# Pooled attention then top-1 experts: other SBUF places for V and scores, Q ahead of K at the start, w2 split after the tokens

## The chip, the cores and the metric

The program runs on one core of a Trainium2 chip. The metric is the device time of one execution in microseconds. Before the change it is 1212.16 us, the median of three runs (1210.98 to 1213.45).

## What is computed

Attention over 8 batches x 8 heads x 1152 tokens x 64, with queries pooled in pairs, then a top-1 mixture of 8 experts over the 4608 pooled tokens. All arrays are float32.

```python
q_pool = q.reshape(B, H, S // 2, 2, D).mean(axis=3)
scores = scale * np.matmul(q_pool, k.transpose(0, 1, 3, 2))
attn = softmax(scores)                     # over the 1152 keys
x = (attn @ v) -> (4608, 512)
e = argmax(x @ w_gate)                     # one expert for a token
out = gate * (np.maximum(x @ w1[e], 0) @ w2[e])
```

## The kernel before, in words

**Attention.** The work goes by pairs of heads: 8 batches x 4 pairs. For a pair, `load_pair` loads K (`kn`), Q (`qn`) and V (`vn`) by SP's queue. Neighbouring queries are added into `qp` (line 491; by POOL, for the first pair by DVE), ACT lays K beside itself as `kp` (line 495), TensorE turns both (lines 512 and 518) into PSUM tiles `st`, and ACT copies these to `kT` and `qT` (lines 524 and 529). The 576 pooled queries are handled in two halves of 288. For each half, `scores` makes 9 chunks of 128 keys: a product into `st` (line 556) and an eviction by DVE to the score tile `s` with the running extreme (line 561). There are two `st` tiles, four `s` tiles and three `vn` tiles. When the 9 chunks are done, DVE and TensorE make one bias of them (lines 582, 579, 585), ACT takes the exponential in three parts (line 589), POOL folds the sums (line 635), and `values` multiplies with V (line 660), after which ACT and DVE put the result in `xT` (lines 665 and 666).

**Routing.** After each batch, `row_sums` and `routing` make the logits from `xT` and the router's weights `wg` (line 735), rank the tokens and write the tokens and lists to DRAM.

**Experts.** The tokens are worked in slots of up to 384: two early slots that are known after the last batch but one, then the 8 experts by rank. For a slot, POOL gathers token rows (line 940), `turn_tokens` weighs them (lines 1100, 1101), transposes them on DVE (`xt`, line 1104) and splits them into a high and a low part (`xh` on ACT, line 1108; `xl` on DVE, line 1063). `split_weights` does the same with w1 and w2, four pieces each (`w1h`, `w2h` on ACT, line 1125; `w1l`, `w2l` on DVE, line 1063). `first_products` (line 1157) and `second_products` (lines 1188, 1218) each do three products for one, and `hh` and `hl` (lines 1164, 1166) are the layer between.

**What sets the order.** The `Flow` class plans all this: each step has an engine, a guessed duration, a key and predecessors; `emit` runs a small event simulation with these guesses and issues the steps in the order that comes out. The engines execute that order strictly, each its own; a step's key only shifts it in the plan.

**Memory.** Attention's `kT`, `qT`, `vn` and `fold` are in the pool `rt`, the score tiles in `sp`; both lie on the right side of SBUF. When the last attention step has been issued, `swap_units` closes these pools and opens those of the experts over the same bytes. A new tile then waits for the last readers of the old tiles that lay there.

**The opening.** SP issues K of the first pair, then Q in two transfers; `WARM` products of ones (line 1261) run on TensorE; ACT's queue issues four small loads of `wg`. The lines on which the order there rests are

```python
k0 = f.carry("SP", 480, lambda: load(kn.t, kb), key + K_LOAD, (), [kn], 2600)
q0 = f.carry("SP", 960, load_q, key + K_LOAD, (), [qn], 2600)
piece(key, [8], [0, 1, 2, 3, 4, 5], done(k1, q1))
piece(key + 4, [0, 1, 2, 3, 4, 5, 6, 7], [], done(k1))
```

Of the kernel before, what the change touches and what calls it, by code (L numbers as in the profile page):

```python
# [9 lines left out]
F32 = mybir.dt.float32  # L10
# [54 lines left out]
FILL = 3  # L65
WARM = 2
SWITCH = 110
CALM, CALM_X = 700, 500
# [198 lines left out]
def kernel(  # L267
# [76 lines left out]
    wg_src = w_gate.rearrange("(a s d) e -> s d a e", s=2, d=D)  # L344
    for s in range(2):
        for half in range(2):
            nc.scalar.dma_start(out=wg[s * D:(s + 1) * D, :, half, (2 * half + s) * NE:(2 * half + s + 1) * NE], in_=wg_src[s])
    rev = const.tile([QP, NE], F32, name="rev")
# [67 lines left out]
    def open_attention(exact, base, pairs, units):  # L416

        o = Pools()
        o.wk = base.enter_context(tc.tile_pool(name="wk", bufs=1 if exact else 2))
        o.ps_m = base.enter_context(tc.tile_pool(name="ps_m", bufs=5 if exact else BANKS, space=PSUM))  # L420
        o.ld = pairs.enter_context(tc.tile_pool(name="ld", bufs=1))
        right = {} if exact else dict(side="right")
        o.rt = units.enter_context(tc.tile_pool(name="rt", bufs=1 if exact else 2, **right))
        o.sp = units.enter_context(tc.tile_pool(name="sp", bufs=2 if exact else UNITS, **right))
        o.ps_s = units.enter_context(tc.tile_pool(name="ps_s", bufs=1 if exact else S_BUFS, space=PSUM))
        o.exact = exact
        o.turned, o.before = [], None
        return o
# [30 lines left out]
    def load_pair(o, f, key, b, hp):  # L459
# [13 lines left out]
        load = lambda out, src: nc.sync.dma_start(out=out, in_=src)  # L473
        k0 = f.carry("SP", 480, lambda: load(kn.t, kb), key + K_LOAD, (), [kn], 2600)
        first = not o.exact and b == 0

        def load_q():
            x.q_loads = [load(qn.t[i * D:(i + 1) * D], qb[i * BL:i * BL + D]) for i in range(2)]

        def load_v():  # L480
            ins = load(vn.t, heads(v, b, hp).rearrange("h (p c) d -> p h c d", p=P))
            if first:
                for other in x.q_loads:
# [3 lines left out]
        q0 = f.carry("SP", 960, load_q, key + K_LOAD, (), [qn], 2600)  # L487
        x.v = f.carry("SP", 480, load_v, key + (-30 if opening else K_V), done(q0) if first else done(o.before), [vn], 2600)
        o.before = x.v
        e, eng, ns = ("DVE", nc.vector, dve) if opening else ("POOL", nc.gpsimd, pool)  # L490
        q1 = f.add(e, ns(2 * NJ * D), lambda: eng.tensor_tensor(  # L491
            qp.t.rearrange("p j h d -> p h j d"), qn.t[:, :, :, 0, :], qn.t[:, :, :, 1, :], ALU.add), key + K_POOL,
            done(q0), [qn, qp])

        k1 = f.add("ACT", act(2 * NC * D), lambda: nc.scalar.copy(kp.t.rearrange("p c h d -> p h c d"), kn.t), key + K_POOL,
                   done(k0), [kn, kp])
        key += K_PIECE
        x.k, x.q = {}, {}

        QH = QP // 2  # L500
        assert QP - D == BL and QH + (D - QH) == D and (1 + NJ) * D <= 512

        def piece(key, ks, qs, after):

            pt = hold_of("st", lambda h: o.ps_s.tile([P, 2, 512], F32, **h.own("st")))
            nk = len(ks)

# [12 lines left out]

            s = f.add("PE", 31 * 2 * (nk + len(qs)), turn, key, after, [pt, *([kT, kp] if ks else []), *([qT, qp] if qs else [])], ROWS)
            o.turned.append(s)
            if ks:
                e = f.add("ACT", act(nk * P) - 44, lambda: nc.scalar.copy(
                    kT.t[:, ks[0] * P:(ks[0] + nk) * P].rearrange("p (c r i) -> p r c i", r=2, i=D),
                    pt.t[:, :, :nk * D].rearrange("p r (c i) -> p r c i", i=D)), key, done(s), [pt, kT])
                x.k.update((c, done(e)) for c in ks)
            if qs:
                e = f.add("ACT", act(NQ) - 44, lambda: nc.scalar.copy(
                    qT.t.rearrange("p (j r i) -> p r j i", r=2, i=QH),  # L530
                    pt.t[:, :, nk * D:(nk + NJ) * D].rearrange("p r (j i) -> p r j i", i=D)[:, :, :, D - QH:]),
                    key, done(s), [pt, qT])
                x.q.update((half, done(e)) for half in range(2))

        piece(key, [8], [0, 1, 2, 3, 4, 5], done(k1, q1))
        piece(key + 4, [0, 1, 2, 3, 4, 5, 6, 7], [], done(k1))
        return x

# [574 lines left out]

    def split_weights(m, f, x, kind, key, step, pool_bits):

# [125 lines left out]
    with ExitStack() as cm, ExitStack() as units, ExitStack() as pairs:  # L1241
# [14 lines left out]
        hold = []  # L1256
        pw = bank(o)

        def warm_up():
            for i in range(WARM):  # L1260
                nc.tensor.matmul(pw.t, ones, ones.unsqueeze(1).broadcast_to([P, 4, P]), start=True, stop=True)

        if WARM:
            f.add("PE", 2900 * WARM, warm_up, -1000, holds=[pw])
        for b in range(B):
# [11 lines left out]
            outs = routing(o, f, key, b, xT, rec, sums, outs, hold)  # L1277
            if b == B - 2:
# [11 lines left out]
        for i, ns in enumerate(((EARLY_N,),) * EARLY + RANKS):  # L1290
# [3 lines left out]
            for j, n in enumerate(ns):  # L1294
# [82 lines left out]
```

## Time and profile before

| what | value |
|---|---|
| median of three runs | 1212.16 us (1210.98 to 1213.45) |
| profiled execution, own time | 1203.37 us |
| its span | 1201.8 us |
| TensorE busy | 1159.8 us, 97% of the span |
| VectorE / ScalarE / GpSimd busy | 783.2 / 636.6 / 848.7 us |
| granted TensorE clock, mean | 0.993 |

Times in rows are microseconds from the span's start. "PE" is TensorE's products, "PEld" its weight loads, "DVE" VectorE, "ACT" ScalarE, "POOL" GpSimd, "SPq" the queue that issues transfers. A bracket at a row's end gives the idle time of that engine before it and what ended it. TensorE's products are pipelined, so the durations of neighbours overlap.

### The profile page before, as it was taken

How to read it: one execution, taken by the hardware profiler on the slowest of the kernel's cores; microseconds unless marked ns; L12 is line 12 of the kernel's file. 1: busy time of each engine (PE TensorE's matmuls, PEld its weight loads, DVE VectorE, ACT ScalarE, POOL GpSimd, SP SyncE). 2: the span in 40 equal slices, each digit the busy share in tenths (PEclk: the TensorE clock that was granted, in tenths of full speed). 3: DMA queues.
4: the chain of work that ended last, by engine and by line, in shares of the span. 5: the costliest groups of instructions: out<-in, count | busy, mean ns of one | idle time of the engine just before them, and what ended most of it. 6: DMA issues, size and time to landing. Idle time of an engine off the chain costs nothing.

```text
span 1201.8 us, 33990 instructions
## 1 busy us (share of the span) xinstructions
PE 1159.8 (97%) x14185; PEld 818.4 (68%) x14185; DVE 783.2 (65%) x2147; ACT 636.6 (53%) x784; POOL 848.7 (71%) x468
## 2 busy tenths in 40 slices
PE   7999999999999999999999998998999999999996
PEld 3555565555565555565555554997898989999985
DVE  5767867867867767877867965984454644536440
ACT  3666666666666567566657555443342433525440
POOL 1989899899899999899999525365666665641010
PEclk9999999999999999999999998999999999999998
DMA  7554525424524433534435333673353434525320
GB/s 195 118 139 112 109 56 144 109 60 115 135 64 122 98 88 102 119 87 124 99 90 125 81 120 96 148 237 113 97 160 90 153 116 129 153 85 185 112 91 20
DMA packets 77491, 138.12 MB, mean 115 GB/s; under 512 B 11274, under 2 KB 34706, under 8 KB 77329
## 3 DMA queue, kind: packets, MB, share of 16 engines
q1 hardware_dynamic: 66528, 116.19, 36.4%
q0 software_dynamic: 9712, 19.64, 5.7%
q8 instruction: 113, 1.85, 0.7%
q14 instruction: 50, 0.40, 0.1%
q10 hardware_dynamic: 1088, 0.03, 0.1%
HBM read 115.04 MB, written 21.02 MB: 113 GB/s over the span
## 4 chain that ended last, share of the span: by engine, by line
PE 46%; POOL 4%; issue 4%; DVE 3%; DMA 2%; ACT 1%; SPq 0%; POOLq 0%; DVEq 0%; ACTq 0%
PE ph L1157 17%; PE py L1218 12%; PE m L660 5%; PE py L1188 5%; PE st L556 5%; POOL fold L635 3%; PE sums L630 1%; DMA qn<-in_q_dram 1%; DVE s L561 1%; POOL qp L491 1%; PE sums L644 1%; DMA xr<-x_runs,ix 0%; PE m L1207 0%; ACT s L589 0%; PE st L512 0%
## 5 line engine op out<-in xcount | busy, mean ns | idle before, releaser
L561 DVE TENSOR_SCALAR_CACHE_REDUCE s<-st 128x576 f32<-128x576 f32 x576 | 419.7, 753 | 156.8 <-PE st L556 152.7
L589 ACT ACTIVATE s<-s,bias 128x1728 f32<-128x1728 f32 x192 | 320.6, 1729 | 167.9 <-DVE bias L585 160.7
L556 PE MATMUL st<-qT,kT 64*64 64x288 f32 x4608 | 364.9, 412 | 8.5 <-DVE s L561 6.9
L660 PE MATMUL m<-s,vn 64*64 64x288 f32 x4608 | 355.8, 405 | 0.0
L556 PEld LDWEIGHTS st<-qT,kT 64*64 64x64 f32 x4608 | 162.2, 133 | 146.5 <-DVE s L561 60.5
L660 PEld LDWEIGHTS m<-s,vn 64*64 64x64 f32 x4608 | 174.3, 133 | 86.5 <-issue 2.6
L635 POOL TENSOR_TENSOR fold<-s 128x1728 f32<-128x1728 f32 x58 | 224.4, 3869 | 7.0 <-ACT s L589 6.8
L635 POOL TENSOR_TENSOR fold<-fold,s 128x1728 f32<-128x1728 f32 x58 | 224.7, 3875 | 1.3
L940 POOL DMA_INDIRECT xr<-x_runs,ix x99 | 109.9, 1110 | 89.5 <-PE st L556 24.9
L1157 PE MATMUL ph<-xh,w1h 128*128 128x384 f32 (+6 forms) x480 | 151.5, 316 | 6.4 <-ACT xh L1108 6.0
L1157 PE MATMUL ph<-xl,w1h 128*128 128x384 f32 (+6 forms) x480 | 150.0, 313 | 1.1 <-DVE xl L1063 1.1
L1157 PE MATMUL ph<-xh,w1l 128*128 128x384 f32 (+6 forms) x480 | 149.5, 311 | 0.0
L1226 POOL DMA_INDIRECT out_dram<-y,rec x41 | 45.6, 1113 | 142.1 <-ACT hh L1164 46.7
L1166 DVE SCALAR_TENSOR_TENSOR hl<-ph,hh 128x384 fp32r<-128x384 f32 (+5 forms) x100 | 54.9, 549 | 107.8 <-ACT hh L1164 107.5
L1164 ACT ACTIVATE hh<-ph 128x384 fp32r<-128x384 f32 (+5 forms) x100 | 48.7, 487 | 133.4 <-PE ph L1157 133.3
L1157 PEld LDWEIGHTS ph<-xh,w1h 128*128 128x128 f32 x480 | 91.4, 190 | 9.3 <-ACT xh L1108 6.5
L1157 PEld LDWEIGHTS ph<-xl,w1h 128*128 128x128 f32 x480 | 91.4, 190 | 2.5 <-DVE xl L1063 1.8
L1157 PEld LDWEIGHTS ph<-xh,w1l 128*128 128x128 f32 x480 | 91.1, 190 | 0.0
L1218 PE MATMUL py<-w2h,hh 128*128 128x512 f32 x224 | 88.6, 395 | 0.0
L1218 PE MATMUL py<-w2h,hl 128*128 128x512 f32 x224 | 88.3, 394 | 0.0
L1218 PE MATMUL py<-w2l,hh 128*128 128x512 f32 x224 | 88.0, 393 | 0.0
L839 POOL DMA_INDIRECT lists<-re,di x48 | 46.2, 962 | 53.0 <-PE m L660 18.5
(186 smaller groups left out, 1464.7 us busy)
## 6 DMA issues: line engine op xcount, KB each, us to landing
raw<-in_moe_w_dram SPq DMA_DIRECT2D x80, 512.0 KB, 4.3
qn<-in_q_dram SPq DMA_DIRECT2D x64, 384.0 KB, 5.7
kn<-in_k_dram SPq DMA_DIRECT2D x32, 576.0 KB, 4.9
vn<-in_v_dram SPq DMA_DIRECT2D x32, 576.0 KB, 4.5
x_runs<-row SPq DMA_DIRECT2D x96, 99.0 KB, 2.1
xr<-x_runs,ix POOLq DMA_INDIRECT x99, 3.2
x_runs<-empty SPq DMA_DIRECT2D x4, 297.0 KB, 10.2
xq<-x_runs,ix POOLq DMA_INDIRECT x49, 2.7
```

The lines of the kernel that those rows point to most:

```text
L556: made = nc.tensor.matmul(pt.t[to, h, :HQ], x.kT.t[up, c * P + i * D:c * P + (i + 1) * D], x.qT.t[up, cols], start=True, stop=True, tile_p ...
L561: nc.vector.tensor_scalar(s.t[:, c], pt.t[:, :, :HQ], -SCALE, None, op0=ALU.mult, op1=ALU.min, accum_out=mx.t[:, c:c + 1],)
L589: nc.scalar.activation(s.t[:, c0:c0 + n], s.t[:, c0:c0 + n], AF.Exp, bias=bias.t, scale=-1.0)
L635: add = lambda to, a, b: nc.gpsimd.tensor_tensor(to, a, b, ALU.add)
L660: made = nc.tensor.matmul(pa[i].t[cs, :HQ], x.vn.t[up, h, c, :], s.t[up, c, h], start=c == 0, stop=c == NC - 1, tile_position=(up.start, c ...
L839: ins = nc.gpsimd.indirect_dma_start(out=lists, out_offset=bass.IndirectOffsetOnAxis(ap=di.t[:, j:j + 1], axis=0), in_=re.t[:, j, :], in_o ...
L940: return nc.gpsimd.indirect_dma_start(out=x.xr[i // NQD].t[:, i % NQD, :], out_offset=None, in_=xg, in_offset=bass.IndirectOffsetOnAxis(ap ...
L1157: made = nc.tensor.matmul(view()[:, i, :], a[:, c, fp], b[:, c, :n], start=c == 0 and k == 0, stop=c == NDC - 1 and k == 2)
L1164: a = f.add("ACT", act(nb * n) - 44, lambda fs=fs, view=view: nc.scalar.activation(hidden(m)[0][:, fs, :n], view(), AF.Relu), at - 20, don ...
L1166: d = f.add("DVE", dve(nb * n), lambda fs=fs, view=view: nc.vector.scalar_tensor_tensor(hidden(m)[1][:, fs, :n], view(), 0.0, hidden(m)[0] ...
L1188: made = nc.tensor.matmul(py.t[:, :n], a[:, c % 2, ds], b[:, c, :n], start=c == 0 and k == 0, stop=c == NFC - 1 and k == 2)
L1218: made = nc.tensor.matmul(py.t[:n], a[:, c, hs], b[:, c % 2, :], start=c == 0 and k == 0, stop=c == NFC - 1 and k == 2)
```

## The change

Five things are changed. (1) The router's weights are loaded by SP after the first pair, not by ACT's queue at the start. (2) The V tiles get a pool of their own, `vp`, opened after the score tiles, and the four score tiles are laid down at once in the order 3, 2, 1, 0. (3) In the first pair, the first half of Q is loaded first, then K in two parts (chunks 0 to 3 and 4 to 8), then Q's second half. The additions of Q, the copies of K, the turns and the copies after them go by the same parts, on DVE, POOL and ACT. (4) Small products of ones fill TensorE's time between these parts. (5) An expert's w2 is split only after its first tokens have been turned.

```diff
+FILL_W, FILL_Q, FILL_K = 2, 3, 2
...
+    def load_router():
...
-            nc.scalar.dma_start(out=wg[...], in_=wg_src[s])
+                nc.sync.dma_start(out=wg[...], in_=wg_src[s])
...
+        o.vp = o.rt if exact else units.enter_context(tc.tile_pool(name="vp", bufs=1, **right))
+        if not exact:
+            for i in reversed(range(UNITS)):
+                o.sp.tile([P, NC, 2, HQ], F32, name=f"s_{i}", bufs=1)
...
-        x.vn = vn = tile_of(o, "vn", [P, 2, NC, D], bufs=3, pool=o.rt)
+        x.vn = vn = tile_of(o, "vn", [P, 2, NC, D], bufs=3, pool=o.vp)
...
+        if opening:
+            parts = slice(0, 4), slice(4, NC)
+            q_in = [f.carry("SP", 1200, lambda: load_q(half_j[0]), key + K_LOAD, (), [qn], 1700)]
+            k_in = [f.carry("SP", 480, lambda cs=cs: load(kn.t[:, :, cs], kb[:, :, cs]), key + K_LOAD + 1 + cs.start, (), [kn], 1300)
+                    for cs in parts]
+            q_in.append(f.carry("SP", 1200, lambda: load_q(half_j[1]), key + K_LOAD + 10, (), [qn], 1700))
+            q1 = [pooled(e, js, done(p)) for e, js, p in zip(("DVE", "POOL"), half_j, q_in)]
+            k1 = [beside("ACT", slice(0, 2), done(k_in[0])), beside("DVE", slice(2, 4), done(k_in[0])), beside("ACT", parts[1], done(k_in[1]))]
+            q0 = q_in[1]
...
+            if fill:
+                f.add("PE", 230 * fill, lambda: o.warm(fill, 1), key, [s] if s else (), [o.pw])
...
+        if opening:
+            piece(key, [], [0, 1, 2], done(q1[0]), FILL_Q)
+            piece(key + 1, [0, 1, 2, 3], [], done(*k1[:2]), FILL_K, True)
+            piece(key + 2, [4, 5, 6, 7, 8], [], done(k1[2]))
+            piece(key + 22, [], [3, 4, 5], done(q1[1]))
...
-                      key + step * j, done(got[j]), [raw[j], w[j]])
+                      key + step * j, [*done(got[j]), *after], [raw[j], w[j]])
...
+        f.add("PE", 3300, lambda: (warm(WARM, 4), warm(FILL_W, 1)), -1000, holds=[o.pw])
...
+                    router = f.carry("SP", 2600, load_router, 1, outs, [], 1500)
...
-                    w.w2, w.w2_ready = split_weights(m, f, w, "w2", at, 10, 0)
+                    w.w2, w.w2_ready = split_weights(m, f, w, "w2", at, 10, 0, x.turned)
```

Line numbers of the changed file are some 30 to 36 higher. Three places where the order of instructions shows it follow.

TensorE at the very start, before (`m` is the bank of the products of ones, `st` a PSUM tile, `kp` and `qp` K and Q ready to be turned):

```order
L1261 MATMUL m_222<-ones 128x512 x2
L512 MATMUL st_232<-ident,kp_230 128x64 x16
L512 MATMUL st_257<-ident,kp_230 128x64 x2
L518 MATMUL st_257<-ident,qp_253 128x48
L518 MATMUL st_257<-ident,qp_253 128x64
...
L556 MATMUL st_278<-qT_276,kT_251 64x288 x4
L556 MATMUL st_283<-qT_276,kT_251 64x288 x4
```

and now (`kp_333` is K of the second pair):

```order
L1297 MATMUL m_225<-ones 128x512 x2
L1297 MATMUL m_225<-ones 128x128 x2
L543 MATMUL st_240<-ident,qp_238 128x48
...
L1297 MATMUL m_225<-ones 128x128 x3
L537 MATMUL st_255<-ident,kp_252 128x64 x8
L1297 MATMUL m_225<-ones 128x128 x2
L592 MATMUL st_270<-qT_250,kT_266 64x288 x4
L592 MATMUL st_275<-qT_250,kT_266 64x288 x4
L537 MATMUL st_286<-ident,kp_252 128x64 x10
...
L592 MATMUL st_335<-qT_250,kT_266 64x288 x4
L543 MATMUL st_344<-ident,qp_238 128x48
...
L537 MATMUL st_352<-ident,kp_333 128x64 x16
L592 MATMUL st_369<-qT_250,kT_266 64x288 x4
```

The first score product now follows half of Q and four chunks of K; the rest of K comes after two products, Q's second half and K of the second pair after eight.

DVE where attention ends and the first slot's tokens are turned, with what each row waits for (`xt` is the transposed token tile, `m_2` the result of the last half but one), before:

```order
L666 TENSOR_TENSOR xT_1_9171<-xT_1_9171,m_2_10080 128x288 [waits PE_49,Activation_49]
L1104 STREAM_TRANSPOSE xt_0_10259<-xr_0_9768 128x4x4x32 [waits DMAHW5_49,PE_49]
L1104 STREAM_TRANSPOSE xt_1_10264<-xr_1_9877 128x4x4x32
L1063 TENSOR_TENSOR w1l0_10262<-raw_0_9713,w1h0_10261 128x1024 [waits DMAHW0_49,Activation_49]
L1063 TENSOR_TENSOR xl_10267<-xt_0_10259,xh_10266 128x4x128 [waits Activation_49]
```

and now:

```order
L702 TENSOR_TENSOR xT_1_9195<-xT_1_9195,m_2_10104 128x288 [waits PE_49,Activation_49]
L1140 STREAM_TRANSPOSE xt_0_10284<-xr_0_9792 128x4x4x32
L1140 STREAM_TRANSPOSE xt_1_10289<-xr_1_9901 128x4x4x32
L1099 TENSOR_TENSOR w1l0_10287<-raw_0_9737,w1h0_10286 128x1024 [waits DMAHW3_49,Activation_49]
L1099 TENSOR_TENSOR xl_10292<-xt_0_10284,xh_10291 128x4x128 [waits Activation_49]
```

The order is the same; the transpose no longer waits for TensorE and a transfer. On ACT the second piece of w1 (`w1h1`) loses its wait for TensorE in the same way.

ACT where the third slot begins (`y` is a result of the slot before, `xh` the high part of the new tokens), before:

```order
L1236 COPY y_11076<-py_11028 128x512
L1125 CAST w2h_11089<-raw_10768 128x1024
L1125 CAST w2h_11102<-raw_10787 128x1024
L1125 CAST w2h_11117<-raw_10859 128x1024
L1236 COPY y_11123<-py_11069 128x512
L1125 CAST w2h_11128<-raw_10921 128x1024
L1108 CAST xh<-xt_11141 128x4x128
```

and now:

```order
L1272 COPY y_11101<-py_11053 128x512
L1272 COPY y_11134<-py_11094 128x512
L1144 CAST xh<-xt_11139 128x4x128
L1161 CAST w2h_11159<-raw_10793 128x1024
L1161 CAST w2h_11162<-raw_10812 128x1024
L1161 CAST w2h_11175<-raw_10884 128x1024
L1200 ACTIVATE hh<-ph_11152 128x384
```

The slot's last token tile is now cast ahead of all four pieces of w2; on DVE its weighing, transpose and low part stand ahead of them likewise.

## Rows read from the trace of the kernel before

**Rows 1.** Stretches: length, busy PE PEld DVE ACT POOL, clock, DMA, GB/s.

```profile
0.00:50.00 50.00, 41.23 (x538) 19.72 (x542) 30.20 (x150) 24.61 (x24) 25.43 (x21) 1.00 0.57 148
...
150.00:200.00 50.00, 49.49 (x842) 29.48 (x842) 33.60 (x98) 31.64 (x30) 49.06 (x19) 1.00 0.36 85
...
700.00:750.00 50.00, 44.76 (x651) 25.18 (x646) 32.01 (x84) 26.59 (x32) 24.72 (x24) 0.95 0.35 105
...
800.00:850.00 50.00, 45.52 (x218) 40.33 (x217) 26.06 (x50) 16.15 (x26) 29.33 (x28) 0.97 0.38 114
```

**Rows 2.** Order of time in the opening: start, duration, engine, line.

```profile
0.97 0.44 SPq L473 DMA_DIRECT2D kn<-in_k_dram  x1
...
1.28 3.78 PE L1261 MATMUL m<-ones 128*128 128x512 f32 x4 [1.28 <-DVE ones L322]
...
5.41 1.15 ACT L495 COPY kp<-kn 128x1152 f32<-128x1152 f32 x1 [2.94 <-DMA kn<-in_k_dram]
...
7.86 1.01 ACT L524 COPY kT<-st 128x1024 f32<-128x1024 f32 x1 [1.30 <-PE st L512]
...
9.84 0.96 DVE L491 TENSOR_TENSOR qp<-qn 128x768 f32<-128x768 f32 x1 [5.48 <-DMA qn<-in_q_dram]
...
10.86 0.91 PE L518 MATMUL st<-ident,qp 48*128 48x48 f32 x12 [2.93 <-DVE qp L491]
...
12.66 5.93 PE L556 MATMUL st<-qT,kT 64*64 64x288 f32 x48 [0.90 <-ACT qT L529]
...
24.18 0.29 DVE L585 TENSOR_REDUCE bias<-st 128x1 f32<-128x128 f32 x1
```

**Rows 3.** Score products on TensorE, 12.6 to 18.7 us: busy, mean ns.

```profile
L556 PE MATMUL st<-qT,kT 64*64 64x288 f32 x48 | 5.9, 637 | 0.9 <-ACT qT L529 0.9
```

**Rows 4.** The same group between 30 and 60 us.

```profile
L556 PE MATMUL st<-qT,kT 64*64 64x288 f32 x212 | 17.6, 412 | 0.4 <-DVE s L561 0.4
```

**Rows 5.** DVE's evictions, 12.6 to 24 us.

```profile
L561 DVE TENSOR_SCALAR_CACHE_REDUCE s<-st 128x576 f32<-128x576 f32 x12 | 8.8, 756 | 4.5 <-PE st L556 4.5
L561 DVE DVE_READ_ACCUMULATOR s<-st 128x1 f32 x11 | 0.9, 83 | 0.0
```

**Rows 6.** Short stretches, columns as in rows 1.

```profile
16.00:18.00 2.00, 2.00 (x24) 0.48 (x20) 1.53 (x5) 0.00 (x0) 0.00 (x0) 1.00 1.04 208
...
745.00:746.00 1.00, 0.55 (x1) 0.29 (x1) 1.00 (x2) 1.00 (x3) 1.00 (x1) 0.50 0.70 228
```

**Rows 7.** Order of time where attention ends.

```profile
739.65 0.94 PE L673 MATMUL sums<-ones 128*128 128x128 f32 x6
739.79 1.30 DVE L1104 STREAM_TRANSPOSE xt<-xr 128x512 f32<-128x512 f32 x2 [5.30 <-PE m L660]
...
742.60 0.39 ACT L675 COPY sm<-sums 128x288 f32<-128x288 f32 x1
...
744.78 0.62 ACT L1108 CAST xh<-xt 128x512 fp32r<-128x512 f32 x1
...
746.98 0.69 PE L1157 MATMUL ph<-xl,w1h 128*128 128x384 f32 x1 [0.84 <-DVE xl L1063]
...
748.88 2.15 PE L735 MATMUL sums<-xT,wg 128*32 128x288 f32 x16
```

**Rows 8.** Transfers of one kind (the page): count, median us from issue to landing.

```profile
xr<-x_runs,ix POOLq DMA_INDIRECT x99, 3.2
```

**Rows 9.** Order of time where the third slot begins.

```profile
812.05 1.00 POOL L940 DMA_INDIRECT xr<-x_runs,ix  x1 [0.30 <-PE py L1218]
...
818.77 0.59 ACT L1236 COPY y<-py 128x512 f32<-128x512 f32 x1 [0.34 <-PE py L1218]
...
822.95 0.57 PE L1157 MATMUL ph<-xh,w1h 128*128 128x384 f32 x1 [4.26 <-ACT xh L1108]
823.73 0.69 PE L1157 MATMUL ph<-xl,w1h 128*128 128x384 f32 x1 [0.22 <-DVE xl L1063]
```

**Rows 10.** All products that read V: duration ns min/median/max.

```profile
L660 PE MATMUL m<-s,vn x4608: 402/403/455, 26.5 to 739.3; 64*64 64x288 f32 x192
```

More of the change, by code (lines that the diff above doesn't have):

```diff
@@ L344 @@
     wg_src = w_gate.rearrange("(a s d) e -> s d a e", s=2, d=D)
-    for s in range(2):
-        for half in range(2):
-            nc.scalar.dma_start(out=wg[s * D:(s + 1) * D, :, half, (2 * half + s) * NE:(2 * half + s + 1) * NE], in_=wg_src[s])
+    def load_router():
+        for s in range(2):
+            for half in range(2):
+                nc.sync.dma_start(out=wg[s * D:(s + 1) * D, :, half, (2 * half + s) * NE:(2 * half + s + 1) * NE], in_=wg_src[s])
     rev = const.tile([QP, NE], F32, name="rev")
@@ L473, in load_pair, with load_q @@
         load = lambda out, src: nc.sync.dma_start(out=out, in_=src)
-        k0 = f.carry("SP", 480, lambda: load(kn.t, kb), key + K_LOAD, (), [kn], 2600)
         first = not o.exact and b == 0
-        def load_q():
-            x.q_loads = [load(qn.t[i * D:(i + 1) * D], qb[i * BL:i * BL + D]) for i in range(2)]
+        x.k, x.q, x.last = {}, {}, []
+        def load_q(js):
+            x.last = [load(qn.t[i * D:(i + 1) * D, :, js], qb[i * BL:i * BL + D, :, js]) for i in range(2)]
         def load_v():
@@ L482, in load_v, with pooled @@
             if first:
-                for other in x.q_loads:
+                for other in x.last:
                     tc.add_manual_dep(ins.ins, other.ins.name, mybir.DependencyInfo(
                         mybir.DependencyClass.Sync, mybir.DependencyReason.DATA), reason="Q is needed sooner")
-        q0 = f.carry("SP", 960, load_q, key + K_LOAD, (), [qn], 2600)
+        def pooled(e, js, after):
+            eng, ns, js = (nc.vector, dve, js) if e == "DVE" else (nc.gpsimd, pool, js)
+            return f.add(e, ns(2 * (js.stop - js.start) * D), lambda: eng.tensor_tensor(
+                qp.t[:, js].rearrange("p j h d -> p h j d"), qn.t[:, :, js, 0, :], qn.t[:, :, js, 1, :], ALU.add),
+                key + K_POOL, after, [qn, qp])
@@ new lines, in beside @@
+        def beside(e, cs, after):
+            copy = nc.scalar.copy if e == "ACT" else nc.vector.tensor_copy
+            return f.add(e, (act if e == "ACT" else dve)(2 * (cs.stop - cs.start) * D), lambda: copy(
+                kp.t[:, cs].rearrange("p c h d -> p h c d"), kn.t[:, :, cs]), key + K_POOL, after, [kn, kp])
+        every_j, half_j = slice(0, NJ), (slice(0, NJ // 2), slice(NJ // 2, NJ))
+        if opening:
[7 more added lines that the diff above has]
+            q0 = q_in[1]
+        else:
+            k0 = f.carry("SP", 480, lambda: load(kn.t, kb), key + K_LOAD, (), [kn], 2600)
+            q0 = f.carry("SP", 960, lambda: load_q(every_j), key + K_LOAD, (), [qn], 2600)
@@ L488, in load_pair @@
         x.v = f.carry("SP", 480, load_v, key + (-30 if opening else K_V), done(q0) if first else done(o.before), [vn], 2600)
         o.before = x.v
[L490 to L496, printed above, removed]
+        if not opening:
+            q1 = pooled("POOL", every_j, done(q0))
+            k1 = beside("ACT", slice(0, NC), done(k0))
@@ L497, in load_pair, with piece @@
         key += K_PIECE
-        x.k, x.q = {}, {}
         QH = QP // 2
         assert QP - D == BL and QH + (D - QH) == D and (1 + NJ) * D <= 512
-        def piece(key, ks, qs, after):
+        def piece(key, ks, qs, after, fill=0, split=False):
             pt = hold_of("st", lambda h: o.ps_s.tile([P, 2, 512], F32, **h.own("st")))
-            nk = len(ks)
+            nk, nq = len(ks), len(qs)
             def turn():
@@ L519, in turn, with keep @@
                                             ident[up, up], tile_position=(up.start, 0))
-            s = f.add("PE", 31 * 2 * (nk + len(qs)), turn, key, after, [pt, *([kT, kp] if ks else []), *([qT, qp] if qs else [])], ROWS)
-            o.turned.append(s)
[L523 to L527, printed above, removed]
+            def keep(e, n0, n1):
+                to = kT.t[:, (ks[0] + n0) * P:(ks[0] + n1) * P].rearrange("p (c r i) -> p r c i", r=2, i=D)
+                src = pt.t[:, :, n0 * D:n1 * D].rearrange("p r (c i) -> p r c i", i=D)
+                nc.scalar.copy(to, src) if e == "ACT" else nc.vector.tensor_copy(to, src)
@@ new lines, in piece @@
+            s = f.add("PE", 31 * 2 * (nk + nq), turn, key, after, [pt, *([kT, kp] if ks else []), *([qT, qp] if qs else [])], ROWS)
+            o.turned.append(s)
+            if fill:
+                f.add("PE", 230 * fill, lambda: o.warm(fill, 1), key, [s] if s else (), [o.pw])
+            for e, n0, n1 in (("ACT", 0, nk // 2), ("DVE", nk // 2, nk)) if split else (("ACT", 0, nk),) if ks else ():
+                e = f.add(e, act((n1 - n0) * P) - 44, lambda e=e, n0=n0, n1=n1: keep(e, n0, n1), key, done(s), [pt, kT])
+                x.k.update((c, done(e)) for c in ks[n0:n1])
@@ L532, in piece @@
                     key, done(s), [pt, qT])
-                x.q.update((half, done(e)) for half in range(2))
-        piece(key, [8], [0, 1, 2, 3, 4, 5], done(k1, q1))
-        piece(key + 4, [0, 1, 2, 3, 4, 5, 6, 7], [], done(k1))
+                x.q.update((j // (NJ // 2), done(e)) for j in qs)
+        if opening:
[3 more added lines that the diff above has]
+            piece(key + 22, [], [3, 4, 5], done(q1[1]))
+        else:
+            piece(key, [8], [0, 1, 2, 3, 4, 5], done(k1, q1))
+            piece(key + 4, [0, 1, 2, 3, 4, 5, 6, 7], [], done(k1))
@@ L1256, with warm @@
         hold = []
[L1257 to L1264, printed above, removed]
+        o.pw = bank(o)
+        def warm(n, w):
+            for i in range(n):
+                nc.tensor.matmul(o.pw.t[:, :w * P], ones, ones.unsqueeze(1).broadcast_to([P, w, P]), start=True, stop=True)
+        o.warm = warm
+        f.add("PE", 3300, lambda: (warm(WARM, 4), warm(FILL_W, 1)), -1000, holds=[o.pw])
         for b in range(B):
@@ L1276 @@
             outs.append(row_sums(o, f, key, sums, done(*summed), rec, sm, b == B - 1))
-            outs = routing(o, f, key, b, xT, rec, sums, outs, hold)
+            outs = routing(o, f, key, b, xT, rec, sums, [*outs, router], hold)
             if b == B - 2:
```

8 lines of the change are left out of this document (4 added, 4 removed).

## The prediction

> **What bounds the kernel now.** I read the stretches first. Within attention TensorE is busy for 49.49 of 50 us and POOL for 49.06; there is next to nothing to win there. TensorE has real holes in three stretches only: 8.8 us in the first 50, 5.2 us between 700 and 750, 4.5 us between 800 and 850, the last two with a granted clock of 0.95 and 0.97 [rows 1]. The change touches these three places, so I read each in order of time, and then the order of instructions for what waits on what. Since TensorE (with POOL) is full between them, I take a microsecond won in a hole as won at the end.
>
> **The opening.** Before, the first score product starts at 12.66: K lands before 5.41, Q only before 9.84, then come the addition (0.96), the turn (0.91) and two copies [rows 2]. The half's bias is ready at 24.47, and only then the exponential, POOL's fold and the product with V can begin. So the bias is the mark by which I measure the gain.
>
> Now half of Q, 384 KB, is in front. K's 576 KB, alone in front, were there 4.4 us after their issue [rows 2]; I take Q's half at 5.2. Its addition is half of 0.96, so 5.7. TensorE's products of ones last from 1.28 to 5.06 in four records of 0.95 [rows 2], a quarter-width product of two records then costs about 0.47, and two of them end at 6.0. Turning half of Q takes half of 0.91, the three fills 1.4, eight turns of K 0.6 (at Q's price of 0.076 each), the two last fills 0.9 while ACT and DVE copy: first score at 9.4 if everything runs at that pace. If TensorE has reached full clock by 6.0, all this is halved and the score starts at 7.7. TensorE then has worked without a break since 1.28, which it had not before, so I take a value nearer the fast end: 8.2.
>
> From there DVE sets the pace with 756 + 83 ns per chunk [rows 5], about 0.84. Eight chunks are evicted by 8.2 + 0.5 + 6.7 = 15.4. Here something new stands in TensorE's queue: the turn of the second pair's K, ahead of the ninth chunk. It needs that K to be loaded and copied (1.15). K of the second pair is issued when the first pair's K has been copied, near 9, and with some 4.4 us [rows 2] it lands near 13.3, so the copy ends at 14.5, 0.9 before the turn could start anyway. The turn (0.7), the ninth chunk (1.35) and the reduction bring us to 17.6. The copy to kT (1.01 [rows 2]) holds the PSUM tile of the next chunk, which ends at 18.5; the bias follows in about 1.1 more, at 19.6. That is 4.8 us ahead of 24.47. **Term: -4.8**, between -2.5 (slow clock throughout) and -6 (score at 7.7, no delay by the PSUM tile).
>
> What the opening does to others is covered. The four loads of the router's weights now stand on SP behind a V load and ahead of the list initialisation and a K load; their four issues cost SP under 3 us. The first reader of these weights is the first routing, past 120 us, and that K load is for a pair some 40 us off. The additional fills lie where TensorE waits for copies. Should their cover go, they cost at most 2.3 us, which is in the slow end above.
>
> Here the clock's own record needs care. The stretch 16 to 18 us reads a granted clock of 1.00 [rows 6], but the score products until 18.7 take 637 ns in the mean [rows 3], against 412 later [rows 4]. The Trainium skill says that on trn2 the recorded events of the clock gate have been observed to be unreliable and are to be cross-checked (TensorE: Matmul & The Clock Gate, in Seeing it yourself). The durations bear it out here; taking the record at its word, the 0.16 us that each of the first six chunks saves by pace would drop out and the sum would be 1 us smaller.
>
> **The end of attention.** Before, DVE stands idle for 5.30 us until 739.79, because the first transposed token tile lies where V lay and waits for TensorE's last products with it [rows 7]. The order of instructions shows this wait gone, and that of ACT's second w1 piece too. What is late next? ACT's copy of the row sums comes ahead of w1's third and fourth pieces and of the slot's third token tile, and it waits for TensorE's last sums, which end at 740.59. Before, it ran at 742.60, held up by the late casts; now it starts at 740.65. The cast of the third tile followed it by 2.18 and took 0.62 [rows 7]: now 742.83 to 743.45. Its low part on DVE (0.7; the queue there has been cleared early) ends at 744.2, and the product that started at 746.98 starts there: 2.75 us.
>
> The clock adds to it. From 745 it read 0.50 [rows 6], 1.2 of its 2.4 GHz, and the five products from 746.98 to 748.88 and the logits (2.15) ran at that rate; at full clock they take half, which saves 0.95 + 1.07 = 2.0. The clock fell only after TensorE had had next to nothing to do since 740.59, that is for more than 4 us. Now the products return at 743.5 to 744.2, so I expect it not to fall. **Term: -4.75**, between -2.75 (it falls all the same) and -5.3 (the whole wait of DVE).
>
> **The third slot.** Before, TensorE ends the second slot at 818.69 and waits until 822.95, then again until 823.73 [rows 9]. The slot's last token tile was not late: the last of its gathers, at 812.05, lands by 815.3 with the median of 3.2 [rows 8, 9]. It stood behind w2 on both DVE and ACT. Now it comes first. On ACT only the result copy at 818.77 (0.59) is ahead, since it waits for TensorE's last product, so the cast runs from 819.3 to 819.9, the low part ends at 820.65, and the product that started at 823.73 starts at 820.75: 3.0 us. A clock of 0.97 over 50 us [rows 1] means some 3 us at half rate; after a pause of 1.3 instead of 4.3 it should not fall, which saves 1.4. **Term: -4.4**, between -3.0 and -4.6.
>
> w2 itself is split some 5 us later, in all ten slots that start an expert. Its readers come only after the 96 matmuls of the slot's first products, which cover it. I cost that at nothing. If an expert's tokens came so late that this cover is gone, the first products would wait for them too.
>
> **The sum.** -4.8 - 4.75 - 4.4 = -13.95. The profiled execution took 1203.37 us in all (span 1201.8), so it would take 1189.4. The three runs have a median of 1212.16, 8.8 above; nothing in the trace says where that lies, so I keep the difference and forecast 1212.2 - 13.95 = **1198.2 us**.
>
> **Rivals.** *The parts cost more than they bring* (0.16). The trace shows no transfer of 256 KB. If each part of the opening took 3.2 us [rows 8], one after the other, Q's half would land near 5, K's parts at 8 and 11, Q's rest at 14.5, the second pair's K past 17. The first scores would start near 10, and TensorE would stand at the early turn of that K until about 18.5, 3 us longer than above. The opening would then gain 1 instead of 4.8: 1202. For it: K and both parts of Q are ahead of it in one queue. Against it: before, K and Q followed each other within 4.4 us of each other, 768 KB. The Trainium skill sides with this rival: a transfer has a fixed cost near 2 us, so one large transfer is to be preferred to several (SBUF — State Buffer, The DMA setup-cost knee). No run here shows how that cost overlaps between transfers.
>
> *The clock falls nevertheless* at the end of attention, or stays low in the opening (0.16). For it: the pause still amounts to some 3 us in pieces. Then 2.0 and up to 2 are lost: about 1201.
>
> *The lead in the opening is taken back in attention* (0.07). POOL is as full as TensorE [rows 1], and its fold starts earlier, but its additions wait for Q of the third pair, whose transfer cannot start before the second is added. If that Q is late, POOL hands on the delay and only the two later terms remain: 1203.
>
> *Slower, by the new places of V and scores* (0.04). If TensorE read V or the scores more slowly where they lie now, all 576 chunks with V would pay. The gains, 14, and 2.4 more are spent at 16.4 / 576 = 28 ns a chunk, 3.6 ns on each of 4608 records; at 6 ns a record the time would be 1226. Against it: these records take 402, 403 and 455 ns at least, in the middle and at most, over three V tiles and four score tiles at different places [rows 10].
>
> *The layout change frees nothing, or the split order is undone by other waits* (0.05): the program's waits show them gone, but the rows that follow might wait for something that was hidden. With the opening alone: 1207.
>
> **How the numbers follow.** The forecast has 0.52: all three terms within their bounds. The rivals have the 0.48 above. Full gains at all ends give -15.9, so 1196; run to run 1.5 us more: low 1194. The high end takes in the first three rivals and the slow ends of all three terms (-2.5 - 2.75 - 3.0 = -8.25, so 1204), and the last case: 1207. A measurement tells 0.2% of the time, 2.4 us, from no change. Faster by more than that: 0.91, all cases but the slow one and odd mixtures; within: 0.05; slower: 0.04.
>
> **What would show it.** First score product at 8 (7.7 to 9.4) and first bias near 19.6; no wait of TensorE at the second pair's K. The first transposed token tile straight after the addition to xT, the row sums' copy at once after TensorE's sums, and a clock of 1.00 there. At the third slot a pause of TensorE of 1.3, with w2's casts behind the token cast. Products with V at 403 ns. I am wrong if TensorE's holes are as long as before, if attention takes longer than before from its first bias to its last product, or if new holes appear at the second products of the later experts.

## The result, and the profile after

The changed kernel takes 1200.55 us (median of four runs, 1200.03 to 1202.09); the kernel before, on the same chip, takes 1211.57. The ratio is 0.9913, 95% interval 0.9901 to 0.9924, so about 11 us are gained where 13.95 were forecast. The level of the kernel before differs from chip to chip (1204 to 1213 us in the four groups of runs here), so each run is compared with the kernel before in its own group, by the ratio. The rows of the kernel before come from an execution of 1203.37 us, at the lower level, and the rows below from one of 1202.09 us on a chip of the higher level; so the lengths of pauses are compared, and not the times at which rows start late in the program.

The stretches of the changed kernel, with the columns of [rows 1]:

```profile
0.00:50.00 50.00, 43.68 (x592) 23.33 (x596) 32.53 (x157) 24.93 (x27) 27.60 (x23) 1.00 0.58 157
150.00:200.00 50.00, 49.50 (x842) 29.50 (x838) 33.54 (x97) 32.75 (x30) 49.06 (x19) 1.00 0.38 92
700.00:750.00 50.00, 47.52 (x700) 28.09 (x690) 30.34 (x81) 26.23 (x29) 23.35 (x23) 0.98 0.33 100
750.00:800.00 50.00, 49.67 (x259) 43.24 (x258) 44.22 (x125) 24.06 (x43) 21.55 (x20) 0.96 0.71 197
800.00:850.00 50.00, 48.48 (x241) 43.14 (x240) 28.01 (x59) 16.98 (x28) 30.88 (x30) 1.00 0.41 125
```

TensorE's holes shrink in all three places: from 8.8 to 6.3 us, from 5.2 to 2.5, from 4.5 to 1.5. The clock is at 1.00 now in the third, but 0.98 and 0.96 on either side of 750 us.

The opening in order of time, which answers to [rows 2]:

```profile
5.38 0.56 DVE L496 TENSOR_TENSOR qp<-qn 128x384 f32<-128x384 f32 x1 [1.01 <-DMA qn<-in_q_dram]
...
7.82 0.41 ACT L502 COPY kp<-kn 128x256 f32<-128x256 f32 x1 [0.72 <-DMA kn<-in_k_dram]
...
9.67 1.20 PE L592 MATMUL st<-qT,kT 64*64 64x288 f32 x16 [0.28 <-ACT kT L549]
...
12.74 0.76 DVE L597 TENSOR_SCALAR_CACHE_REDUCE s<-st 128x576 f32<-128x576 f32 x1 [0.84 <-PE st L592]
...
21.54 0.29 DVE L621 TENSOR_REDUCE bias<-st 128x1 f32<-128x128 f32 x1
```

Q's half is there by 5.38, near the 5.2 of the forecast, but K's first part only by 7.82; the first score product starts at 9.67 instead of 12.66 and the bias is ready at 21.83 instead of 24.47.

The end of attention in order of time, which answers to [rows 7]:

```profile
738.65 1.30 DVE L1140 STREAM_TRANSPOSE xt<-xr 128x512 f32<-128x512 f32 x2
...
743.89 0.94 PE L709 MATMUL sums<-ones 128*128 128x128 f32 x6
744.86 0.40 ACT L711 COPY sm<-sums 128x288 f32<-128x288 f32 x1 [3.32 <-PE m L696]
...
745.31 0.68 PE L717 MATMUL sums<-sums_of,sm 128*96 128x16 f32 x6 [0.49 <-issue]
...
747.72 0.69 PE L1193 MATMUL ph<-xh,w1h 128*128 128x384 f32 x1 [1.73 <-ACT xh L1144]
...
748.45 0.69 PE L1193 MATMUL ph<-xl,w1h 128*128 128x384 f32 x1
...
750.34 2.15 PE L771 MATMUL sums<-xT,wg 128*32 128x288 f32 x16
```

The transposed token tile no longer waits for TensorE: it starts five microseconds before TensorE's last products of ones, which L709 is. From the end of these to the product with the low part there are 748.45 - 744.83 = 3.62 us, where the kernel before had 746.98 - 740.59 = 6.39. But the clock falls all the same, and the logits still take 2.15. The granted clock by short stretches (length, busy PE, granted clock, DMA, GB/s):

```profile
746.00:747.00 1.00, 0.00 (x0) 1.00 1.07 407
747.00:748.00 1.00, 0.28 (x1) 0.79 0.48 124
748.00:749.00 1.00, 0.96 (x3) 0.50 0.35 65
...
754.00:755.00 1.00, 1.00 (x7) 0.80 0.86 303
```

The third slot, which answers to [rows 9]:

```profile
821.81 0.58 ACT L1272 COPY y<-py 128x512 f32<-128x512 f32 x1 [4.97 <-DMA xr<-x_runs,ix]
822.29 0.62 ACT L1144 CAST xh<-xt 128x512 fp32r<-128x512 f32 x1
...
822.96 0.44 PE L1193 MATMUL ph<-xh,w1h 128*128 128x384 f32 x1 [1.24 <-ACT xh L1144]
823.69 0.44 PE L1193 MATMUL ph<-xl,w1h 128*128 128x384 f32 x1 [0.28 <-DVE xl L1099]
```

The pause is 1.24 where it was 4.26, and the products run at full clock (0.44 instead of 0.69). The products with V, over the whole program (busy, mean ns), are not slower at the new places [rows 10]:

```profile
L696 PE MATMUL m<-s,vn 64*64 64x288 f32 x4608 | 356.5, 405 | 0.0
```

### The profile page after: what moved, and what is told of

The parts are those of the page before. It is cut to its first block, busy times and chain, and to the rows that moved or that the text cites. A ratio compares the mean times of both kernels' runs of the same rounds, so it can differ in the third digit from the quotient of the medians.

```text
span 1200.5 us, 34022 instructions
## 1 busy us (share of the span) xinstructions
PE 1163.5 (97%) x14199; PEld 819.5 (68%) x14199; DVE 785.4 (65%) x2149; ACT 636.6 (53%) x786; POOL 851.3 (71%) x469
## 4 chain that ended last, share of the span: by engine, by line
PE 46%; issue 4%; POOL 3%; DVE 3%; ACT 2%; DMA 1%; POOLq 0%; DVEq 0%; ACTq 0%
PE ph L1193 16%; PE py L1254 11%; PE m L696 6%; PE st L592 5%; PE py L1224 5%; POOL fold L671 2%; PE sums L666 1%; DVE s L597 1%; ACT s L625 1%; PE sums L680 1%; DMA qn<-in_q_dram 1%; PE m L1243 0%; POOL xr L976 0%; POOL qp L496 0%; DVE row L859 0%
```

## The experiments

Twelve runs were made in three groups, each group on one chip with the kernel before beside it. The first group takes the change apart, the second asks what stands behind the lost part of the gain, the third goes back to the kernel before and takes the fills out of the opening. "Measured" is the ratio to the kernel before in the same group, with its 95% interval in brackets.

**The kernel before once more.**

> The kernel before, unchanged, for a trace beside the changed one's on the same chip. Theory (three holes, each part of the change closes its own): the ratio is 1.000 within 0.1%, and the profile's attention, from the first bias to TensorE's last sums, takes some 715 us as in the first trace of before (24.5 to 739.7), so that the whole is near 1203. Rival (attention runs at varying speed, and the first trace of before was a quick one): the profiled time is near 1210, and the 7 to 8 us lie between the first bias and the last sums.

Measured: 0.9998 [0.9989, 1.0007]. Two copies of one kernel agree within 0.1%. From the first bias (24.62) to the start of the last products of ones (738.95) this execution takes 714.3 us, as the theory has it; the first trace of the kernel before had 715.2.

**The opening alone.** The changed kernel with the places and w2's order as before:

```diff
-        x.vn = vn = tile_of(o, "vn", [P, 2, NC, D], bufs=3, pool=o.vp)
+        x.vn = vn = tile_of(o, "vn", [P, 2, NC, D], bufs=3, pool=o.rt)
-                    w.w2, w.w2_ready = split_weights(m, f, w, "w2", at, 10, 0, x.turned)
+                    w.w2, w.w2_ready = split_weights(m, f, w, "w2", at, 10, 0)
```

(and the four score tiles are not laid in advance).

> Only the opening (router's loads moved, Q ahead of K in parts, fills). Three holes: 2.6 us less than before, which is what the first bias came earlier in the changed trace, ratio 0.9978. Rival (the lead is taken back in attention): ratio 0.9995 to 1.0005, with the lead gone by the second batch's logits.

Measured: 0.9967 [0.9957, 0.9978], which is 4.0 us of 1204.6, between 2.7 and 5.2. Its profile has K's first part at 6.29 and the bias at 20.78, 3.8 us ahead of the kernel before on the same chip (24.62):

```profile
20.50 0.28 DVE L617 TENSOR_REDUCE bias<-st 128x1 f32<-128x128 f32 x1
```

The 2.6 of the first profile came from an execution in which that part was late. What the order of the loads, the parts and the moved router loads bring each was not taken apart.

**The places alone**, in the kernel before:

```diff
+        o.vp = o.rt if exact else units.enter_context(tc.tile_pool(name="vp", bufs=1, **right))
+        if not exact:
+            for i in reversed(range(UNITS)):
+                o.sp.tile([P, NC, 2, HQ], F32, name=f"s_{i}", bufs=1)
-        x.vn = vn = tile_of(o, "vn", [P, 2, NC, D], bufs=3, pool=o.rt)
+        x.vn = vn = tile_of(o, "vn", [P, 2, NC, D], bufs=3, pool=o.vp)
```

> Only the places of V and scores. Three holes: TensorE's pause at the end of attention is 2.8 us shorter, the clock falls there all the same, ratio 0.9977. Rival (the clock stays up): 4.8 us, 0.996. Rival (products with V run at another speed): more than 0.5% either way, and another mean than 405 ns of these products.

Measured: 0.9969 [0.9958, 0.9980], 3.7 us (2.4 to 5.1). In its order of time the end of attention is that of the changed kernel, step by step:

```profile
739.59 0.94 PE L677 MATMUL sums<-ones 128*128 128x128 f32 x6
...
740.56 0.40 ACT L679 COPY sm<-sums 128x288 f32<-128x288 f32 x1 [3.32 <-PE sums L677]
...
743.42 0.69 PE L1161 MATMUL ph<-xh,w1h 128*128 128x384 f32 x1 [1.73 <-ACT xh L1112]
```

**w2 behind its tokens alone**, in the kernel before:

```diff
-                    w.w2, w.w2_ready = split_weights(m, f, w, "w2", at, 10, 0)
+                    w.w2, w.w2_ready = split_weights(m, f, w, "w2", at, 10, 0, x.turned)
```

> Only w2 split after the first tokens are turned. Three holes: TensorE's pause at the third slot falls from 4.3 us to 1.3, the clock stays up there, 4.4 us in all, ratio 0.9964. Rival (the later split costs at the later experts): under 2 us, with new pauses of TensorE ahead of second products.

Measured: 0.9968 [0.9956, 0.9980], 3.9 us (2.4 to 5.3). The third slot's first product has the same wait and duration as in the changed kernel:

```profile
822.73 0.44 PE L1157 MATMUL ph<-xh,w1h 128*128 128x384 f32 x1 [1.24 <-ACT xh L1108]
```

The later experts pay nothing for it: in this trace, as in the kernel before, TensorE has no idle time ahead of the second products, which read w2. The three parts together are 4.0 + 3.7 + 3.9 = 11.6, and the three ratios multiply to 0.9904, where the whole gave 0.9913 and, in the next run, 0.9919. With intervals of about 0.1% on each part, none is seen to help or hinder another.

**The changed kernel once more, in the second group.**

> The changed kernel as it is, on the same chip as the three below. All theories: 0.991 of the kernel before, as the first time; the three parts apart gave 0.9967, 0.9969 and 0.9968 on another visit, whose product is 0.9904, so if the parts don't help or hinder one another the ratio lies between 0.990 and 0.992. In its profile the hole from the last sums to the first expert product's low half again about 3.6 us, the TensorE clock again down to 0.50 behind it.

Measured: 1193.98 us, 0.9919 [0.9905, 0.9932]. The end of attention is as expected: 3.6 us from the last products of ones to the product with the low part, and a granted clock of 0.50 from 740 to 746 us. The opening of this execution, with K's first part in time:

```profile
6.27 0.29 DVE L502 COPY kp<-kn 128x256 f32<-128x256 f32 x1 [0.51 <-DMA kn<-in_k_dram]
...
8.50 1.20 PE L592 MATMUL st<-qT,kT 64*64 64x288 f32 x16 [0.29 <-ACT kT L549]
...
20.37 0.29 DVE L621 TENSOR_REDUCE bias<-st 128x1 f32<-128x128 f32 x1
```

**Fills in the hole.** Six more products of ones behind the turn of the sums (`HOLE = 6`):

```diff
         p = f.add("PE", 500, turn, key, done(p), [sm, sums])
+        if end:
+            f.add("PE", 215 * HOLE, lambda: [nc.tensor.matmul(
+                sums.t[:, 3 * P:], ones, ones, start=True, stop=True) for _ in range(HOLE)], key, done(p), [sums])
```

> The changed kernel with six more all-ones products (128x128, some 0.3 us each) between the turn of the sums and the first expert product, where TensorE stands idle for 1.73 us in the changed kernel's profile just before its clock falls. Theory (the clock falls because TensorE has nothing to do in this hole): it stays at 1.00 from 744 to 755 us, products of 0.34 us instead of 0.52 from the start, about 2 us faster than the changed kernel. Rival (the clock falls whatever stands in this hole, by what came before it): the same drop, no difference, or up to 0.4 us slower where the fills outlast the wait.

Measured: 1191.98 us, 0.9899 [0.9884, 0.9914], 2.0 less than the changed kernel beside it. Its order of time where attention ends:

```profile
739.58 1.58 PE L729 MATMUL sums<-ones 128*128 128x128 f32 x12
...
741.46 0.45 PE L1197 MATMUL ph<-xh,w1h 128*128 128x384 f32 x1 [0.29 <-ACT xh L1148]
...
743.26 1.18 PE L775 MATMUL sums<-xT,wg 128*32 128x288 f32 x16
```

With work in the hole the granted clock reads 1.00 throughout, the first product takes 0.45 instead of 0.69 and the logits 1.18 instead of 2.15. So the idle hole is what let the clock fall, and the fall costs 2.0. The rival, that it falls whatever stands there, is out. The Trainium skill (Perfetto Trace Analysis, Matmul Optimizations) says that TensorE scales its power with how much it is used and that its products should therefore come back to back; the trace agrees, with these 2.0 us.

**No fills behind the last products.** The three products of ones behind the last products with V (L709), fills that nobody reads, are left out:

```diff
-FILL = 3
+FILL = 0
```

> The changed kernel without the three all-ones products behind the last products with V; they write a part of the sums' bank that nothing reads, but ScalarE's copy of the sums stands behind them. Theory (that copy, at 744.86 in the changed kernel's profile, waits for these fills alone, though the sums themselves ended near 739.2): the copy moves to about 741.5, the two weight casts and the cast of the tokens behind it move with it, the first expert product stands at about 0.7 us after the last product with V instead of 3.8 us, so 3 us less, and with the hole gone the clock stays up, 2 us less again: 5 us faster than the changed kernel. Rival (the copy waits for the whole bank of sums for another reason, or a weight that is not there yet takes the wait's place): the product waits as long for something else, 0 to 1 us faster. Second rival (the fills keep the clock up, and without them it falls sooner): 0 to 2 us slower.

Measured: 1188.75 us (1187.43 to 1190.62), 0.9872 [0.9857, 0.9887], 5.2 less than the changed kernel beside it. Order of time:

```profile
733.95 0.39 ACT L711 COPY sm<-sums 128x288 f32<-128x288 f32 x1
...
736.40 0.68 PE L717 MATMUL sums<-sums_of,sm 128*96 128x16 f32 x6
...
736.93 0.42 PE L1193 MATMUL ph<-xh,w1h 128*128 128x384 f32 x1
...
738.28 0.44 PE L1193 MATMUL ph<-xl,w1h 128*128 128x384 f32 x1 [0.93 <-DVE xl L1099]
```

The copy of the sums now runs 2.5 us ahead of the end of the products with V, and not 0.9 behind it. The fills write columns 384 to 511 of the tile `sums`, the copy reads 0 to 287; that it waited for them all the same shows that the wait set by the program goes by the tile, not by its columns. The casts behind the copy come with it, the hole all but closes, and the clock stays at 1.00 without any filling. This is the fastest version here: it beats both kernels.

**The same in the kernel before.**

```diff
-FILL = 3
+FILL = 0
```

> The kernel before without the three all-ones products at the end of attention. In the changed kernel their removal gave 5 us. Theory (before the change they were covered: the copy of the sums came 2 us after them, held up by casts that wait for the late token tile, and only the change made them the last thing waited for): no difference from the kernel before, 0 to 0.5 us either way, the copy of the sums still near 2 us behind the last product with V. Rival (the fills were worth removing in any case): 3 to 5 us faster than before.

Measured: 1.0004 [0.9994, 1.0014]. Order of time:

```profile
747.19 1.31 DVE L1104 STREAM_TRANSPOSE xt<-xr 128x512 f32<-128x512 f32 x2 [5.18 <-PE m L660]
...
750.00 0.39 ACT L675 COPY sm<-sums 128x288 f32<-128x288 f32 x1
```

Without the change the fills cost nothing: the copy stands behind casts that wait for the token tile. The 5 us became available only through the change.

**V's places alone**, and **the score tiles' places alone**, in the kernel before:

```diff
-        if not exact:
-            for i in reversed(range(UNITS)):
-                o.sp.tile([P, NC, 2, HQ], F32, name=f"s_{i}", bufs=1)
```

```diff
-        x.vn = vn = tile_of(o, "vn", [P, 2, NC, D], bufs=3, pool=o.vp)
+        x.vn = vn = tile_of(o, "vn", [P, 2, NC, D], bufs=3, pool=o.rt)
```

(each against the places of both).

> The kernel before with V's tiles in the pool of their own, but the score tiles where they were. The places of both together gave 0.9969. By the program's waits, V's new places free the first transposed token tile of TensorE, but ScalarE's first w1 cast now has a wait for TensorE, which neither before nor with both places it has. Theory (both are needed, because that cast stands ahead of the cast of the tokens in ScalarE's queue and waits for the last products with the scores): the first expert product is as late behind the last sums as before, some 6 us, and the time within 1 us of before. Rival (V's places do it all, the cast's wait is over in time): the hole half as long, 3 to 4 us faster, as with both.

> The kernel before with the score tiles at the new places, V where it was. By the program's waits only ScalarE's second w1 cast is freed of TensorE, the transposed token tile still waits for the last products with V. Theory (the token tile is what ends the hole): DVE still stands idle until the last products with V, everything behind it as before, no difference, 0.5 us faster at best. Rival (the weight casts end the hole): 2 to 4 us faster.

Measured: 0.9997 [0.9988, 1.0006] for V, 0.9998 [0.9988, 1.0008] for the scores. Neither half brings anything, both together brought 3.7 us in the first group. With V's places alone, the token tile is early but a weight cast holds ScalarE. Its row names no releaser, but it starts 0.08 us after TensorE's last product with V (746.57), for which the program makes it wait:

```profile
741.47 1.30 DVE L1105 STREAM_TRANSPOSE xt<-xr 128x512 f32<-128x512 f32 x2
...
746.65 1.05 ACT L1126 CAST w1h<-raw 128x1024 fp32r<-128x1024 f32 x1 [5.58 <-issue]
747.60 1.14 ACT L1109 CAST xh<-xt 128x512 fp32r<-128x512 f32 x2
```

With the scores' places alone, that cast is early and the token tile waits:

```profile
747.54 1.30 DVE L1107 STREAM_TRANSPOSE xt<-xr 128x512 f32<-128x512 f32 x2 [5.04 <-PE m L663]
```

**K's second part held back** until the first is in (`x.parts` holds the two loads):

```diff
+            if len(x.parts) == 2:
+                tc.add_manual_dep(x.parts[1].ins, x.parts[0].ins.name, mybir.DependencyInfo(
+                    mybir.DependencyClass.Sync, mybir.DependencyReason.DATA), reason="the first part is needed sooner")
```

> The changed kernel with the load of K's second part (and with it all that SyncE issues later: Q's second half, the next K, V) held back until K's first part is in. Theory (the first part, 256 KB, is late, at 7.8 us in the profile, because the transfers issued right behind it share the engines with it): it is in by about 6.0 to 6.5 us, the first score product at about 8.3 instead of 9.67, the first bias about 1 us sooner, and the whole 1 us faster at best, which the time can hardly tell; the profile's first copy of K tells it. Rival (it is late by the transfers ahead of it and its own latency): it lands no sooner, the second part lands 2 to 3 us later than now, and the first bias is 1 to 2 us later.

Measured: 1195.72 us, 0.9935 [0.9921, 0.9948], 1.7 slower than the changed kernel beside it. Order of time:

```profile
6.04 0.29 DVE L510 COPY kp<-kn 128x256 f32<-128x256 f32 x1
...
6.78 1.65 PE L1305 MATMUL m<-ones 128*128 128x128 f32 x6
...
8.36 0.69 PE L545 MATMUL st<-ident,kp 64*128 64x64 f32 x8
...
10.13 1.41 PE L600 MATMUL st<-qT,kT 64*64 64x288 f32 x16
```

K's first part is there by 6.04, no sooner than in the early ones of the executions without the hold (5.89 at the earliest), and this kernel is the slower one, so holding does not pay. K's turn was late here because three fills ahead of it took 1.65 instead of 1.06. Whether the transfers behind it are what sometimes delays the first part stays open: in seven executions with the changed opening it was there by 5.89, 6.04, 6.27 and 6.29, or at 7.82, 7.93 and 8.17.

**No fills in the opening**, on top of the version without fills at the end:

```diff
-FILL_W, FILL_Q, FILL_K = 2, 3, 2
+FILL_W, FILL_Q, FILL_K = 0, 0, 0
```

> The changed kernel without the fills at the end (0.9872 of before) and now without the narrow all-ones products of the opening too. Theory (they keep TensorE at full clock while it waits for Q and K): without them the clock falls in the opening to 0.50 as in the kernel before, the first score product comes at 8.2 to 8.6 as with them, but the chunks until the fifth or so come slower, and the first bias 0.5 to 1.5 us later: 0.988 of before. Rival (they stand in the way of K's turn and the clock would not matter, since DVE's evictions set the pace): the bias 0 to 0.4 us sooner, 0.987 or a little less.

Measured: 1201.31 us, 0.9907 [0.9892, 0.9922], against 0.9872 [0.9857, 0.9887] with them. Order of time:

```profile
7.93 0.41 ACT L502 COPY kp<-kn 128x256 f32<-128x256 f32 x1 [0.96 <-DMA kn<-in_k_dram]
...
10.01 2.20 PE L592 MATMUL st<-qT,kT 64*64 64x288 f32 x16 [0.93 <-ACT kT L549]
...
23.16 0.29 DVE L621 TENSOR_REDUCE bias<-st 128x1 f32<-128x128 f32 x1
```

The first score products take 2.20, near half the pace of the 1.20 above, and from K's arrival to the bias there are 15.5 us; in the first profile of the change, where K came equally late, 14.0. That is 1.5 us for the fills in this pair of executions. But the execution with the fills in the hole, which has all the fills of the opening and K at 8.17, shows that they do not always hold the clock: TensorE stood idle for 1.41 us between the fills and K's turn, the granted clock read 0.50 from 9 to 12 us, and the first score products were slow too:

```profile
10.36 2.05 PE L593 MATMUL st<-qT,kT 64*64 64x288 f32 x16
```

There it is 15.0 us from K to the bias, so the fills bring 0.6 to 1.5 us of the opening when K is late. The rival, a bias that is not later without them, is out. The ratios differ by 4.2 us, more than that. Of the rest, the trace shows 2.6 to 2.9 in attention: from the first bias to the start of the last products with V it takes 719.8 us, against 716.9 to 717.3 in the three other kernels of this group. Why is not shown, nor whether it has to do with the fills.

## Why the prediction was right, and where it was off

**The direction and the range held**: 1200.55 in 1194 to 1207. All three holes shrank, by the mechanisms given. The median is 2.4 us above the forecast; the traces name 2.8, of which 0.8 lie in the opening and 2.0 at the end of attention.

**The opening, -4.8 forecast: -4.0 alone** (measured 2.7 to 5.2, bounds -2.5 to -6). The first score product comes at 8.50 to 8.66 where K is in time, against 8.2. The sum has no term for the landing of K's first part; where that is late (7.82 and 8.17 with the fills), the first score product comes at 9.67 and 10.36. What was missed behind it is mainly one step: "eight chunks are evicted" at DVE's pace of 0.84. The third chunk waits 0.84 more (the row at 12.74), because the turn of K's second part stands in TensorE's queue ahead of it and needs one of the two `st` tiles. From first score to bias there are 20.66 - 8.50 = 12.2 us, where 11.4 were reckoned. The second pair's K, feared as a new wait, was copied at 14.07 in the first profile and turned at 17.58 without a wait on it.

**The end of attention, -4.75 forecast: -3.7 alone** (measured 2.4 to 5.1). The wait was forecast to shrink by 2.75 and shrank by 2.77, and what is late next is what the text named: the copy of the row sums behind TensorE's last sums. The clock's 2.0 is the step that failed: "I expect it not to fall". It fell after two pauses of 0.49 and 1.73 us with only 0.68 of small products between, so the comparison with the 4 us of before was no ground. It also rested on a single execution: in the second trace of the kernel before the clock reads 0.59 already between 742 and 743 us, where TensorE had been idle since 739.89. The rival that had the clock fall nevertheless was right, at this place; the size of 2.0 was right too, as the fills in the hole gave back just that. The text also took "TensorE's last sums" as needed by the copy. They are fills that nobody reads: the copy could have run at once, and this was worth another 5 us.

**The third slot, -4.4 forecast: -3.9 alone** (measured 2.4 to 5.3). The pause is 3.0 shorter and the clock stays up, as reckoned, and the later split of w2 costs nothing, as assumed.

**The rivals.** That parts cost more than they bring is out as a whole: it had 1 us for the opening. But its landing of K's first part near 8 does occur, in three of the seven executions, 1.5 to 2 us late; with the fills the bias is then ready at 21.83 or 23.13 instead of 20.66 to 20.81. The Trainium skill's advice of one large transfer in place of several (SBUF — State Buffer, The DMA setup-cost knee) spoke for this rival; the measured 4.0 us for the opening speak against it here. Whether the late first parts are a price of splitting stays open. Places of V and scores make nothing slower: 405 ns in the mean. The lead of the opening is not taken back in attention: the opening alone keeps its 4.0. One sign of being wrong did show, attention that takes longer from its first bias to its last product (722.1 us against 715.2 in the first two traces), but it goes with the chip and not with the change, as the last section shows.

## What to carry to other kernels

When a wait is removed, look at what the next one is for: a filler that was free behind the old wait can become the new bound, as it wrote to a tile that another engine was about to read. A wait that two tiles' places cause on two engines shows no gain until both are moved, so a half tried alone says nothing. After an engine's pause has been shortened, ask what the clock does in the rest of it; a handful of products that nobody reads gave back 2 us, and no pause at all gave more.

## What the runs showed that was not expected

The record of the clock and the pace of the products disagree in the opening. Of the kernel before, one execution reads 1.00 through the whole of its first score products, at 16 to 18 us for one [rows 6], another 0.50 from 9 to 18 us (columns: length, busy PE, clock, DMA, GB/s), with the first score products at much the same pace, 637 [rows 3] and 691 ns:

```profile
10.00:12.00 2.00, 0.90 (x12) 0.50 0.78 225
12.00:14.00 2.00, 1.62 (x16) 0.50 1.00 283
```

```profile
L556 PE MATMUL st<-qT,kT 64*64 64x288 f32 x48 | 6.4, 691 | 0.9 <-ACT qT L529 0.9
```

So the durations, not the record, are to be read there. The time of the same kernel also differed by 0.7% between chips, much of it in attention: from the first bias to the last products of ones the changed kernel took 722.1 us beside its first measurement and 715.6 in the second group. The kernel before with the places of V or of the scores alone took 721.5 and 721.8 in the third group, where the level was again 1212, and the runs of the first two groups that have these products, changed or not, 714.3 to 715.7. So this part goes with the chip, and its 6 to 7 us are most of the 8.8 by which the first trace of the kernel before lay under its median. Nothing in these runs says what differs between the chips.
